# A fused attention and MLP kernel on one core: q and k cast by loads of GpSimd's queue, two more groups with seven quarter products, and a list planned anew

## The chip, the cores and the metric

The kernel runs on one core of a Trainium2 chip. The core has TensorE (PE; matmuls, with the weight load PEld beside them), VectorE (DVE), ScalarE (ACT), GpSimd (POOL) and SyncE (SP, which here only issues DMAs). Each takes its instructions in order, and they wait for each other by semaphores. Sixteen DMA engines move data between HBM and the on-chip memory SBUF; the loads are issued from the queues of SP, ACT and POOL. PSUM is the memory that TensorE writes. The metric is device microseconds of one execution; lower is better.

## The reference

Attention with a feature map, then an MLP with a residual. `phi` takes the largest magnitude off and gives two exponentials; the MLP normalises, multiplies by `w_ch1`, clips at zero, multiplies by `w_ch2`.

```python
def phi(x):                                  # x: 8 x 8 x 576 x 64
    proj = np.einsum('bhsd,df->bhsf', x, w_phi)          # 128 features
    proj = proj - np.max(np.abs(proj), axis=-1, keepdims=True)
    return np.concatenate([np.exp(proj), np.exp(-proj)], axis=-1)
q_p, k_p = phi(q), phi(k)
kv, z = np.einsum('bhsf,bhsd->bhfd', k_p, v), np.sum(k_p, axis=2)
num = np.einsum('bhsf,bhfd->bhsd', q_p, kv)
den = np.einsum('bhsf,bhf->bhs', q_p, z)[..., None] + 1e-06
x = (num / den) heads side by side                        # 8 x 576 x 512
xn = (x - mean) / np.sqrt(var + 1e-06) * g_ln
out = x + np.maximum(xn @ w_ch1, 0.0) @ w_ch2             # 512 -> 2048 -> 512
```

## The kernel before

Attention goes in 32 units of two heads of a batch each (units 0 to 31, eight to a pair of batches). A unit needs q, k and v as float32 from HBM: eight token tiles of 128 in the main part, and a ninth, mixed one from the tails of both heads. The main parts lie in three buffers `qk_100`, `qk_102`, `qk_104` (and `v_101`, `v_103`, `v_105`) of two units each, the tails in `qx_88`/`qx_89` and `vx_106`/`vx_107` of four units each.

TensorE needs q and k transposed and in bf16. For units 0 to 7 it transposes them itself. From unit 8 on `a_trans_dma` casts them to bf16 into one of three buffers `b16` (b_0, b_1, b_2, by the unit's number modulo 3), in two steps, `cast_mixed` for the tails and `cast_main` for the rest, on VectorE, ScalarE or GpSimd as the list says; then SyncE issues a transposing DMA into one of four buffers `qkT` (141 to 144). Then follow for each unit the projections `pm` and `pt`, the maxima `m`, the exponentials `ea` and `eb`, the scaled values `vv` (GpSimd: three instructions, lines 1101 to 1107), the product `kv` in the PSUM bank `n_bank` (lines 1162 and 1168), the numerators `num`, and the quotients `x` and `xs` (GpSimd).

The MLP goes in nine groups of four token tiles (0 to 8; `LAST` is 8), each as soon as its `x` is there. The first product `hT_ps` (`first`, and `first_half` in group 0) runs over 16 blocks of 128 of the 2048 features; each is clipped into `hT`. The second product of a group has two forms. `second` (line 1562) adds 16 blocks of 512 columns for each of four token tiles into one PSUM bank: 64 matmuls of 512 columns. `fast` (line 1698) is for the groups in `FAST`: a pair of token tiles by two halves of the columns would be eight quarter products, and it forms seven, from sums of `hT` blocks (`token_sums`, S1 to S4 of each pair) and of `w2` blocks (`weight_sums`, T1 to T4): 7 steps of 16/2 = 8 matmuls of 256 columns for each of two pairs, 112 in all. Each step's sum is read and added into the output tile `o` by VectorE (line 1707). With `second` a tile's result is one instruction, on VectorE (line 1570) or on ScalarE with a residual on GpSimd (lines 1575 and 1579). T lies in the buffers of q and k of units that are past, S likewise, for the second pair in those of v. Before, `FAST` is groups 6, 7 and 8.

The weights come by four loads of GpSimd's queue that cast them to bf16, each half a matrix (1 MB as written): two of `w1` (`w_132`, 4 KB rows), two of `w2` (`w_133`, 2 KB rows). The first loads of `w1` are gated on v of units 2 and 3; SyncE's loads for units 8 and up wait until the second half of `w1` has landed (`hold`).

What sets the order is a list of numbers for each engine, `ORDER`. `Order.run` plays the recorded steps against this list with assumed durations and lags, which decides how the engines' instructions interleave, and where TensorE is given filler matmuls (`wz`, of no use but to keep its clock up) in the first 75 us. The list was made by a planner that used the same assumed figures: `SLACK` (lags and a factor for DMAs), `LAG`, and in `dma` the time of a packet and the lag from its move to its landing.

Of the kernel before, what the change touches and what calls it, by code (L numbers as in the profile page):

```python
# [17 lines left out]
def bcast(ap: bass.AP, dim: int, n: int) -> bass.AP:  # L18
# [10 lines left out]
SLACK = ((0.22, 0.0, 0.0, 0.97), (0.35, 0.6, 1.6, 0.97), (0.22, -1.15, 0.0, 1.07))  # L29
# [36 lines left out]
    """,  # L66
    "SP": """
# [11 lines left out]
    """,  # L79
    "ACT": """  # L80
# [307 lines left out]
def kernel(  # L388
# [46 lines left out]
    BW = 4
# [1776 lines left out]
```

## Time and profile before

| | us |
|---|---|
| median of 3 runs | 354.47 |
| the runs | 352.18, 354.47, 355.43 |
| the profiled execution | 353.76 |
| its span, first to last instruction | 352.0 |
| mean granted clock of TensorE | 0.998 |

The rows that the prediction shows are not shown here. In a group's row stand the line, the engine, the operation, what it writes and reads, the shapes, the count, then busy time in us and the mean of one in ns, then the engine's idle time ahead of it and what ended that. In the chain of waits and in the timeline a row has the start and the duration in us. A row of stretches has for each engine its busy time and the number of its instructions in brackets.

### The profile page before, as it was taken

The page shows a single profiled execution, that of the slowest core. Times are in us where ns is not written, and L with a number is a line of the kernel's source. Part 1 is how long each engine was busy: PE and PEld are TensorE (multiplying, and loading weights), DVE is VectorE, ACT ScalarE, POOL GpSimd, SP SyncE. Part 2 cuts the span into 40 slices and gives each one's busy share as a digit, 9 for nine tenths or more (in the row PEclk, how much of TensorE's full clock was granted, in tenths as well). Part 3 has the DMA queues.
Part 4 walks back from the last instruction along what each step waited for, and adds up shares of the span by engine and source line. Part 5 has one row for each costly group of instructions (what it writes and reads, how often), then busy time and mean ns, then how long its engine had stood idle before and what let it go on. Part 6 is the DMA issues. An engine that isn't in the chain of part 4 may idle for free.

```text
span 352.0 us, 9056 instructions
## 1 busy us (share of the span) xinstructions
PE 339.7 (97%) x3482; PEld 216.1 (61%) x3482; DVE 296.1 (84%) x670; ACT 253.5 (72%) x561; POOL 192.7 (55%) x250
## 2 busy tenths in 40 slices
PE   8887998999999999999999999999999999999995
PEld 7766785655555555464555455555555578488884
DVE  5799984999889889878896799799768699999994
ACT  4997988878999887869776958798676840554410
POOL 5487367849952584667292696987668630000000
PEclk9999999999999999999999999999999999999999
DMA  7999999994997939859809993705061123500053
GB/s 206 277 297 214 212 236 232 254 198 58 266 270 183 248 96 216 160 105 209 281 16 190 284 281 64 136 0 125 10 128 58 62 67 61 148 33 3 7 114 119
DMA packets 93675, 53.87 MB, mean 153 GB/s; under 512 B 61104, under 2 KB 88048, under 8 KB 93632
## 3 DMA queue, kind: packets, MB, share of 16 engines
q1 hardware_dynamic: 89392, 47.72, 57.2%
q0 software_dynamic: 3328, 4.49, 7.4%
q10 hardware_dynamic: 912, 1.08, 0.9%
q8 instruction: 27, 0.44, 0.5%
q14 instruction: 16, 0.13, 0.1%
HBM read 36.77 MB, written 9.44 MB: 131 GB/s over the span
## 4 chain that ended last, share of the span: by engine, by line
PE 82%; DMA 8%; DVE 3%; issue 2%; POOL 2%; ACT 2%; SPq 1%; ACTq 0%; POOLq 0%
PE hT_ps L1530 27%; PE ch_ps L1562 23%; PE ch L1698 10%; DMA w<-in_moe_w_ch_dram 6%; PE pm L1017 4%; PE n_bank L1168 4%; PE sum L1881 3%; PE num L1226 3%; PE pt L1026 2%; DMA qk<-in_q_dram 2%; POOL vv L1101 1%; PE n_bank L1162 1%; PE n_bank L1226 1%; ACT ea L914 1%; PE n_bank L1232 1%
## 5 line engine op out<-in xcount | busy, mean ns | idle before, releaser
L1530 PE MATMUL hT_ps<-xT,w 128*128 128x512 bf16 x432 | 103.9, 380 | 0.0
L1562 PE MATMUL ch_ps<-w,hT 128*128 128x512 bf16 x384 | 89.7, 380 | 1.2 <-DMA w<-in_moe_w_ch_dram 1.2
L1101 POOL TENSOR_TENSOR vv<-v,ek 128x1024 bf16<-128x1024 f32 x32 | 61.2, 1912 | 49.6 <-issue 32.9
L1074 DVE TENSOR_REDUCE m<-pm 128x8 f32<-128x1024 f32 x60 | 72.3, 1214 | 14.2 <-PE pm L1017 13.1
L1094 ACT ACTIVATE eb<-pm 128x1024 bf16<-128x1024 f32 x64 | 64.5, 1044 | 4.8 <-DVE m L1074 3.0
L1138 ACT ACTIVATE ea<-pt 128x1024 bf16<-128x1024 f32 x56 | 56.1, 1045 | 11.1 <-PE pt L1026 10.9
L1530 PEld LDWEIGHTS <-w 128*128 128x128 bf16 x432 | 38.1, 97 | 39.2 <-issue 1.9
L1562 PEld LDWEIGHTS <-hT 128*128 128x128 bf16 x384 | 35.0, 97 | 39.8 <-issue 2.5
L1540 ACT ACTIVATE hT<-hT_ps 128x512 bf16<-128x512 f32 x64 | 37.7, 608 | 18.6 <-PE hT_ps L1530 18.4
L1293 POOL TENSOR_TENSOR x<-numc,rden 128x128 bf16<-128x128 f32 (+1 forms) x56 | 33.6, 615 | 18.6 <-DVE rden L1260 18.6
L1538 DVE TENSOR_SCALAR hT<-hT_ps 128x512 bf16<-128x512 f32 x44 | 29.7, 679 | 5.4 <-PE hT_ps L1530 5.2
L1226 PEld LDWEIGHTS <-ea 128*128 128x128 bf16 x448 | 21.6, 97 | 8.5 <-issue 0.3
L804 POOL TENSOR_TENSOR b<-qk,one 128x1024 bf16<-128x1024 f32 x13 | 24.5, 1890 | 2.3 <-DMA v<-in_v_dram 2.3
L1168 PE MATMUL n_bank<-vv,eb 128*128 128x65 bf16 x512 | 23.8, 194 | 0.0
L1168 PEld LDWEIGHTS <-eb 128*128 128x128 bf16 x512 | 21.3, 98 | 2.2
L1248 DVE TENSOR_TENSOR numc<-num,em 128x390 f32<-128x390 f32 (+1 forms) x32 | 17.0, 530 | 6.6 <-PE num L1226 5.9
L1434 DVE BATCH_NORM_STATS2 st<-x 128x6 f32<-128x512 bf16 (+1 forms) x40 | 21.9, 567 | 0.4 <-POOL x L1293 0.4
L1017 PE MATMUL pm<-wbk,qkT 64*128 64x128 bf16 x448 | 19.9, 218 | 0.2 <-DVE xT L962 0.2
L1107 POOL TENSOR_TENSOR vv<-vx,ek 128x260 bf16<-128x260 f32 x32 | 19.9, 623 | 0.0
L1017 PEld LDWEIGHTS <-qkT 64*128 64x128 bf16 x448 | 13.8, 94 | 9.6 <-issue 6.5
L1579 POOL TENSOR_TENSOR o<-o,x 128x512 f32<-128x512 f32 x13 | 15.0, 1158 | 7.8 <-ACT o L1575 6.9
L1254 DVE TENSOR_TENSOR numc<-numc,num 128x390 f32<-128x390 f32 (+1 forms) x32 | 17.0, 533 | 0.7
(180 smaller groups left out, 659.7 us busy)
## 6 DMA issues: line engine op xcount, KB each, us to landing
out_dram<-o SPq DMA_DIRECT2D x29, 256.0 KB, 3.1
qk<-in_q_dram SPq DMA_DIRECT2D x12, 512.0 KB, 5.6
qk<-in_k_dram SPq DMA_DIRECT2D x12, 512.0 KB, 6.4
v<-in_v_dram SPq DMA_DIRECT2D x12, 512.0 KB, 5.2
w<-in_moe_w_ch_dram POOLq DMA_DIRECT2D x4, 1024.0 KB, 10.4
qk<-in_k_dram SPq DMA_DIRECT2D x8, 256.0 KB, 6.1
qk<-in_q_dram SPq DMA_DIRECT2D x7, 256.0 KB, 5.9
v<-in_v_dram SPq DMA_DIRECT2D x7, 256.0 KB, 6.7
```

Of the source, the lines that this page charges most:

```text
L1017: nc.tensor.matmul(ps[:, half * 4 + c, :], u["qkT"][rows, cols], wbk[rows, half, :], start=True, stop=True,)
L1074: nc.vector.reduce_max(out=m, in_=ps, axis=AX.X, apply_absolute_value=True)
L1094: nc.scalar.activation(eb, ps, AF.Exp, scale=(1.0, -1.0)[t])
L1101: eng.tensor_tensor(out=u["vv"][:, :, 0:MX, 0:D], in0=bcast(vb[:, hh, :].rearrange("p (c d) -> p c d", d=D), 1, 2), in1=bcast(e[:, :, 0:MX ...
L1138: nc.scalar.activation(u["EA"][:, t, 0:1024], u["pt"], AF.Exp, scale=(1.0, -1.0)[t])
L1168: nc.tensor.matmul(ps[:, t, c // 4, :], EB[:, t, c, :], vv[:, t, c, :], start=False, stop=(t == 0 and c == MX - 1), skip_group_check=True,)
L1226: nc.tensor.matmul(ps[t][:, i, :], ea(u, t, c), KV[:, t, c // 4, :], start=True, stop=True,)
L1293: eng.tensor_tensor(out=dst, in0=src, in1=by, op=ALU.mult)
L1530: nc.tensor.matmul(st["ps"], w1_sb[:, kc, jj * P : (jj + 1) * P], xT_bufs[g % XB][:, kc::KC, :], start=(kc == 0), stop=(kc == KC - 1),)
L1540: nc.scalar.activation(h_sb, st["ps"], AF.Relu)
L1562: nc.tensor.matmul(ch[g, i], hT[g, jj][:, i * P : (i + 1) * P], w2_sb[:, jj, :], start=(jj == 0), stop=(jj == JC - 1),)
L1698: nc.tensor.matmul(sums(), left(c), right(c), start=(begin and c == 0), stop=(c == CP - 1), skip_group_check=True,)
```

## The change

Five things change.

First, from unit 8 on the main parts of q and k aren't loaded as float32 any more. `cast_main` goes, and two loads of GpSimd's queue for each unit, one for q and one for k (`load_cast`, line 830 of the new kernel), read 1 KB rows from HBM, cast them and write `b16` directly: 48 loads that read 256 KB each. SyncE's 24 loads of q and k for those units go. The tails are still loaded by SyncE and cast by `cast_mixed`. A `b16` buffer can only be loaded again when the transposing DMA of the unit three before has read it.

Second, `FAST` is groups 4 to 8. In groups 4 and 5 (`lean`) one pair is worked through after the other with a single set S, and its sums lie in two PSUM banks of the pool B: chains 0 and 1 share a bank, chain 2 has the other. In groups 6 to 8 nothing changes in this.

Third, a token sum can be done by GpSimd too, and the list gives it 44 of them.

Fourth, the planner's figures: DMA landings and transposes are assumed later (`SLACK`), the weights' loads land 4.4 and 4.7 us after they moved where it was 2.9, and their pieces move one load after the other.

Fifth, the whole list is planned anew; the first steps that differ are GpSimd's eighth and SyncE's fourteenth.

```diff
-SLACK = ((0.22, 0.0, 0.0, 0.97), (0.35, 0.6, 1.6, 0.97), (0.22, -1.15, 0.0, 1.07))
+SLACK = ((0.22, 0.6, 0.8, 1.0), (0.35, 1.2, 2.2, 1.0), (0.22, -1.15, 0.0, 1.07))
...
     "POOL": """
-        0 7 9 10 20 22 31 86 109 168 131 150 200 219 136 137 206 155 205 241 288 33 246 169 293
+        0 7 9 10 20 22 31 447 449 456 442 86 109 137 170 150 33 131 223 204 136 156 210 209 245
...
-    FAST = (LAST - 2, LAST - 1, LAST)
+    FAST = range(4, LAST + 1)
+    FULL = LAST - 2
...
-            packets, ns, lag = nbytes / row / 16, (0.155 if row == 4096 else 0.084), 2.9
+            packets, ns, lag = nbytes / row / 16, {4096: 0.155, 2048: 0.084}.get(row, 0.048), {4096: 4.4, 2048: 4.7}.get(row, LAND)
...
-        def cast_main(engine):
-            cast(
-                engine, b16[:, 0 : MX * P].rearrange("p (i f) -> p i f", i=2),
-                qk_bufs[u["g"] % NBUF][:, :, u["hh"], :],
+        def load_cast(i):
+            b, h, step = heads(u["pair"], u["i"], 0)
+            t = (q, k)[i]
+            nc.gpsimd.dma_start(
+                out=b16[:, i * 4 * P : (i + 1) * 4 * P].rearrange("p (a f) -> p a f", a=2),
+                in_=bass.AP(
+                    tensor=t.tensor, offset=t.offset + (b * H + h) * S * D,
+                    ap=[[4 * D, P], [S * D, 2], [1, 4 * D]],
+                ),
             )
...
-        add(("DVE", "ACT", "POOL"), (1.13, 0.937, 1.852), rank, cast_main, r=[*loaded(u, "q"), *loaded(u, "k")],
-            w=[("b16", n % NB16)])
-        dma("SP", rank, 0, turn, r=[("b16x", n % NB16), ("b16", n % NB16)],
+        for i in range(2):
+            dma("POOL", rank, 262144, lambda i=i: load_cast(i), w=[("b16" + "qk"[i], n % NB16)], us=0.7, row=1024)
...
+        dma("SP", rank, 0, turn, r=[("b16x", n % NB16), ("b16q", n % NB16), ("b16k", n % NB16)],
...
-                add("DVE", Port(0.335), (), lambda i=i, f=sums: f(i),
+                add(("DVE", "POOL"), (Port(0.335), 1.08), (), lambda e, i=i, f=sums: f(i, e),
...
+        lean = g < FULL
+        z = 0 if lean else p
...
+        if lean:
+            cols, bank = chain % 2 * FH, chain // 2
...
+        if lean:
+            took = ("B", 1) if i in (0, 3) and cs[0] == 0 else None
+            gave = ("B", 1) if i in (5, 6) else None
...
-    def fast_steps():
+    def fast_steps(lean=False):
         pairs_, h1, h2 = range(NM // 2), range(SH), range(SH, CP)
+        if lean:
+            return [
+                (p, i, cs) for p in pairs_
+                for i, cs in [(i, cs) for cs in (h1, h2) for i in range(2)]
+                + [(i, range(CP)) for i in range(2, 7)]
+            ]
...
-                for key in "kqv":
+                for key in "kqv" if m < QK_DMA else "v":
                     load_main(key, m + i, 1 if m < H else HG, rank, "SP")
```

Three places show what moves. The first is the start of GpSimd's queue, after the load of `gln`. Before, the first `vv` (units 0 and 1) follow:

```order
L658 DMA gln<-in_moe_g_ln_dram 128x4x1
L1101 TENSOR_TENSOR vv<-v_101,ek 128x2x8x64
L1106 CAST vv<-ek 128x2x8
L1107 TENSOR_TENSOR vv<-vx_106,ek 128x2x130
L1101 TENSOR_TENSOR vv<-v_101,ek 128x2x8x64
```

Now, at the same place:

```order
L670 DMA gln<-in_moe_g_ln_dram 128x4x1
L830 DMA b_0_145<-in_q_dram 128x2x256
L830 DMA b_0_145<-in_k_dram 128x2x256
L830 DMA b_1_146<-in_k_dram 128x2x256
L830 DMA b_2_147<-in_k_dram 128x2x256
L1118 TENSOR_TENSOR vv<-v_101,ek 128x2x8x64
```

Four cast loads (q and k of unit 9, k of units 10 and 8) stand ahead of all `vv` and of the four loads of the weights.

The second place is where the loads of `w2` are issued, with SyncE's queue at the same time. GpSimd before, from the first half of `w2` on (`vv` of units 4 and 5, then the second half, then a cast of unit 8):

```order
L688 DMA w_133<-in_moe_w_ch_dram 128x8x512
L986 TENSOR_TENSOR x<-xT_140 128x2x2x64
L1101 TENSOR_TENSOR vv<-v_105,ek 128x2x8x64
L1106 CAST vv<-ek 128x2x8
L1107 TENSOR_TENSOR vv<-vx_107,ek 128x2x130
L1101 TENSOR_TENSOR vv<-v_105,ek 128x2x8x64
L1106 CAST vv<-ek 128x2x8
L1107 TENSOR_TENSOR vv<-vx_107,ek 128x2x130
L688 DMA w_133<-in_moe_w_ch_dram 128x8x512
L804 TENSOR_TENSOR b_2_147<-qk_102,one 128x1024
```

GpSimd now:

```order
L700 DMA w_133<-in_moe_w_ch_dram 128x8x512
L1003 TENSOR_TENSOR x<-xT_140 128x2x2x64 x2
L1011 TENSOR_TENSOR xs<-xT_140 128x64
L700 DMA w_133<-in_moe_w_ch_dram 128x8x512
L1118 TENSOR_TENSOR vv<-v_105,ek 128x2x8x64
L1123 CAST vv<-ek 128x2x8
L1124 TENSOR_TENSOR vv<-vx_107,ek 128x2x130
L830 DMA b_2_147<-in_q_dram 128x2x256
L1118 TENSOR_TENSOR vv<-v_105,ek 128x2x8x64
```

The second half of `w2` moves ahead of `vv` of units 4 and 5, and the last load that unit 8 needs, its q, stands behind it. SyncE before, from v of unit 6 on (`v_101` is v of units 6 and 7 here, and the second one is unit 7's; the transposing DMA at the end is unit 8's):

```order
L577 DMA v_101<-in_v_dram 128x2x256
L577 DMA vx_106<-in_v_dram 64x4x64
L577 DMA qk_102<-in_q_dram 128x4x256
L577 DMA qx_88<-in_k_dram 64x4x64 x2
L577 DMA v_101<-in_v_dram 128x2x256
L577 DMA qx_88<-in_q_dram 64x4x64
L577 DMA qx_89<-in_k_dram 64x4x64
L577 DMA qk_102<-in_k_dram 128x4x256
L577 DMA qx_88<-in_q_dram 64x4x64
L577 DMA v_103<-in_v_dram 128x4x256
L823 DMA_TRANSPOSE qkT_141<-b_2_147 128x9x128
```

SyncE now:

```order
L589 DMA v_101<-in_v_dram 128x2x256
L589 DMA qx_88<-in_k_dram 64x4x64 x2
L589 DMA qx_88<-in_q_dram 64x4x64 x2
L840 DMA_TRANSPOSE qkT_141<-b_2_147 128x9x128
L589 DMA qx_89<-in_q_dram 64x4x64
L589 DMA v_101<-in_v_dram 128x2x256
L589 DMA vx_106<-in_v_dram 64x4x64
L589 DMA qx_89<-in_q_dram 64x4x64
L589 DMA vx_106<-in_v_dram 64x4x64
L840 DMA_TRANSPOSE qkT_142<-b_0_145 128x9x128
L589 DMA v_103<-in_v_dram 128x4x256
```

Unit 8's transpose now stands ahead of v of unit 7 and of v of unit 8.

The third place is VectorE at the second product of group 4. Before, a token tile's result of 512 columns stands among maxima (`m`) and statistics of attention:

```order
L1451 TENSOR_SCALAR xc_137<-x,mv 128x512
L1613 TENSOR_TENSOR qk_104<-w_133 128x1024
L1570 SCALAR_TENSOR_TENSOR o<-ch_ps,rstd,x 128x512
L1074 TENSOR_REDUCE m_118<-pm 128x2x4
L1074 TENSOR_REDUCE m_119<-pm 128x2x4 x2
L1570 SCALAR_TENSOR_TENSOR o<-ch_ps,rstd,x 128x512
```

Now (`ch_3979` and `ch_4047` are the two banks of the first pair, `ch_4101` the first of the second pair; each row on `ch` is the result of a step of 8 matmuls):

```order
L1091 TENSOR_REDUCE m_118<-pm 128x2x4
L1737 SCALAR_TENSOR_TENSOR o<-ch_3979,rstd,x 128x256
L866 TENSOR_REDUCE m_118<-n_bank 128x2
L1737 SCALAR_TENSOR_TENSOR o<-ch_4047,rstd,x 128x256
L1737 SCALAR_TENSOR_TENSOR o<-ch_3979,rstd,o 128x256
L1655 TENSOR_TENSOR qk_100<-hT 128x512 x3
L1737 SCALAR_TENSOR_TENSOR o<-ch_4101,rstd,x 128x256
L1737 SCALAR_TENSOR_TENSOR o<-ch_4047,rstd,o 128x256
```

A result of a bank now has to be read before the next but one step of TensorE, which adds to it.

More of the change, by code (lines that the diff above doesn't have):

```diff
@@ L561, in dma @@
             add(queue, took[0], rank, emit, r=r, w=(key, *w), acquire=lanes)
-            add(kind, took[1], rank, None, r=(key, *r), w=(*w, key), lag=1.45, release=lanes)
+            add(kind, took[1], rank, None, r=(key, *r), w=(*w, key), lag=1.9, release=lanes)
             return
-        add(queue, us, rank, emit, r=r, w=(key, *w), acquire=lanes, load=(kind, packets * ns))
+        wide_ = kind == "DMA_w" and pieces > 1
+        line = ["weights issued"] if wide_ else []
+        add(queue, us, rank, emit, r=r, w=(key, *w, *line), acquire=lanes, load=(kind, packets * ns))
+        for i in range(pieces if wide_ else 0):
+            add(kind, Move(packets / pieces, ns), rank, None, r=(key,), w=("weights moved", (key, "moved")))
+        if wide_:
+            add(kind, Move(0.01, ns), rank, None, r=(key, (key, "moved"), *r), w=(*w, key), lag=lag, release=lanes)
+            return
         for i in range(pieces):
@@ L827, in a_trans_dma @@
         rank = rk("trans", n)
-        add(("DVE", "ACT", "POOL"), (0.193, 0.189, 0.357), rank, cast_mixed, r=[*loaded(u, "q"), *loaded(u, "k")],
-            w=[("b16x", n % NB16)])
-        add(("DVE", "ACT", "POOL"), (1.13, 0.937, 1.852), rank, cast_main, r=[*loaded(u, "q"), *loaded(u, "k")],
-            w=[("b16", n % NB16)])
-        dma("SP", rank, 0, turn, r=[("b16x", n % NB16), ("b16", n % NB16)],
+        for i in range(2):
+            dma("POOL", rank, 262144, lambda i=i: load_cast(i), w=[("b16" + "qk"[i], n % NB16)], us=0.7, row=1024)
+        add(("DVE", "ACT", "POOL"), (0.193, 0.189, 0.357), rank, cast_mixed,
+            r=[*loaded(u, "q")[2:], *loaded(u, "k")[2:]], w=[("b16x", n % NB16)])
+        dma("SP", rank, 0, turn, r=[("b16x", n % NB16), ("b16q", n % NB16), ("b16k", n % NB16)],
             w=[("qxT", j), ("qkT", j, 0), ("qkT", j, 1), *[("T", j, i) for i in range(3)]], tiles=NT)
@@ L1617, in weight_sums, with token_sums @@
                     + [("T home", i // 2)], w=[("T2", i, c)])
-    def token_sums(g, c):
-        for p in range(NM // 2):
+    def token_sums(g, c, only=None):
+        for p in range(NM // 2) if only is None else (only,):
+            z = p if g >= FULL else 0
             def blocks(i, odd, p=p):
@@ L1625, in blocks, with sums @@
                 return space[:, s : s + 2 * SH - 1 : 2, (2 * p + i) * P : (2 * p + i + 1) * P]
-            def sums(i, p=p, blocks=blocks):
-                S1, S2, S3, S4 = [t[:, c : c + SH] for t in S_of[p]]
+            def sums(i, engine, z=z, blocks=blocks):
+                S1, S2, S3, S4 = [t[:, c : c + SH] for t in S_of[z]]
                 out_, a, b, op = (
@@ L1634, in sums @@
                 )[i]
-                nc.vector.tensor_tensor(out=out_, in0=a, in1=b, op=op)
+                eng = nc.vector if engine == "DVE" else nc.gpsimd
+                eng.tensor_tensor(out=out_, in0=a, in1=b, op=op)
             for i, reads in ((0, ()), (1, (0,)), (3, (1,)), (2, ())):
-                add("DVE", Port(0.335), (), lambda i=i, f=sums: f(i),
+                add(("DVE", "POOL"), (Port(0.335), 1.08), (), lambda e, i=i, f=sums: f(i, e),
                     r=[hkey[g, jj] for jj in range(2 * c, 2 * c + 2 * SH)]
-                    + [("S", p, j, c) for j in reads] + [("S home", p)], w=[("S", p, i, c)])
+                    + [("S", z, j, c) for j in reads] + [("S home", z)], w=[("S", z, i, c)])
     def fast(g, p, i, cs):
         t0, t1 = 2 * p, 2 * p + 1
+        lean = g < FULL
+        z = 0 if lean else p
         f1, f2 = slice(0, FH), slice(FH, DM)
@@ L1692, in products @@
         def products():
-            if split and i < 2 and cs[0] == 0:
+            if lean:
+                if i in (0, 3) and cs[0] == 0:
+                    ch[g, p, bank] = room_for("B")
+            elif split and i < 2 and cs[0] == 0:
                 ch[g, p, i] = room_for((tag0, tag1)[i])
@@ L1699, in products @@
                     sums(), left(c), right(c),
-                    start=(begin and c == 0), stop=(c == CP - 1), skip_group_check=True,
+                    start=(begin and c == 0 and not (lean and i == 1)), stop=(c == CP - 1), skip_group_check=True,
                 )
@@ L1715, in fast @@
         else:
-            r += [("S", p, s_key, c) for c in range(cs[0], cs[-1], SH)]
+            r += [("S", z, s_key, c) for c in range(cs[0], cs[-1], SH)]
         if t_key is None:
@@ L1748, in fast @@
             dma("SP", counts["V"], 262144, lambda: store(g, t, ch["o", g, t]), r=both)
-    b16_home = [[("b16x", i), ("b16", i)] for i in range(NB16)]
+    b16_home = [[("b16x", i), ("b16q", i), ("b16k", i)] for i in range(NB16)]
     qkT_home = [
@@ L1994, in moe @@
             weight_sums()
+        if g == FULL:
+            add("SP", 0.0, RELU, None, w=[*S_home[1], ("S home", 1)])
         if g == LAST:
@@ L2011, in moe @@
             if g - 1 in FAST:
-                steps = fast_steps()
+                steps = fast_steps(g - 1 < FULL)
                 until = min(len(steps), -(-(jj + 1) * len(steps) // 8))
-                for step in steps[done:until]:
-                    fast(g - 1, *step)
+                for step in range(done, until):
+                    if g - 1 < FULL and 2 * step == len(steps):
+                        for c in (0, SH):
+                            token_sums(g - 1, c, 1)
+                    fast(g - 1, *steps[step])
                 done = until
             if g in FAST and jj in (SH * 2, JC - 1):
-                token_sums(g, 0 if jj < JC - 1 else SH)
+                token_sums(g, 0 if jj < JC - 1 else SH, 0 if g < FULL else None)
             if g - 1 in FAST:
```

5 lines of the change are left out of this document (3 added, 2 removed), and 216 rows, old and new, of the table ORDER.

## The prediction

> **What bounds the kernel now.** I read the page's first part, then busy time by stretches, then TensorE's own waits, then the chain of waits. The page opens with the span and each engine's busy time:
>
> ```profile
> span 352.0 us, 9056 instructions
> PE 339.7 (97%) x3482; PEld 216.1 (61%) x3482; DVE 296.1 (84%) x670; ACT 253.5 (72%) x561; POOL 192.7 (55%) x250
> ```
>
> Busy time by stretches (start and end in us, then each engine, the granted clock, the DMA share):
>
> ```profile
> core 0: us, PE busy (x) PEld busy (x) DVE busy (x) ACT busy (x) POOL busy (x), PEclk, DMA share, GB/s
> 30.00:40.00 10.00, 7.88 (x113) 6.33 (x112) 9.96 (x28) 8.61 (x18) 6.20 (x10) 1.00 1.12 194
> 60.00:285.00 225.00, 224.99 (x2258) 122.59 (x2256) 188.74 (x397) 181.27 (x397) 152.80 (x190) 1.00 0.66 155
> ```
>
> TensorE's waits on the weights (us in total, times, longest):
>
> ```profile
> PE ch_ps L1562 <- DMA w<-in_moe_w_ch_dram: 1.2, 1, 1.2
> PE hT_ps L1387 <- DMA w<-in_moe_w_ch_dram: 0.6, 1, 0.6
> ```
>
> There are two regimes. From 60 to 285 us TensorE works 224.99 of 225 us at full clock (1.00), and nobody else is full: there the time is TensorE's work and nothing else. Before 60 us TensorE is short of work, VectorE is near full, and the DMA share stands above 1, that is, packets queue at all 16 engines. The two waits on the weights are early; no wait of TensorE is longer, and these are the ones that the change can reach. So the change is worth what it takes from TensorE's work, plus or minus what it does to those first 60 us, plus any new wait in the full stretch.
>
> **The change, part by part.**
>
> Second products. Two groups (4 and 5) change from 64 matmuls of 512 columns to 112 of 256 each.
>
> In the chain of waits (start, duration, what) 16 of the old kind take 3.45 us, so a group takes 4 x 3.45 = 13.80:
>
> ```profile
> 219.53 3.45 PE ch_ps L1562 x16
> ```
>
> The new kind already stands there for another group, 112 in 12.23:
>
> ```profile
> 285.39 12.23 PE ch L1698 x112
> ```
>
> Saved: 2 x (13.80 - 12.23) = **3.1 us**, all on the path, since TensorE has no gap there.
>
> What it adds elsewhere, by groups of instructions (busy, mean ns):
>
> ```profile
> L1707 DVE SCALAR_TENSOR_TENSOR o<-ch,rstd,o 128x256 f32<-128x256 f32 x18 | 8.2, 476 | 1.7 <-PE ch L1698 1.7
> ...
> L1635 DVE TENSOR_TENSOR qk<-hT 128x512 bf16<-128x512 bf16 x10 | 4.1, 417 | 0.0
> ...
> L1613 POOL TENSOR_TENSOR qk<-w,qk 128x1024 bf16<-128x1024 bf16 x4 | 8.5, 2123 | 0.0
> ...
> L1579 POOL TENSOR_TENSOR o<-o,x 128x512 f32<-128x512 f32 x13 | 15.0, 1158 | 7.8 <-ACT o L1575 6.9
> ...
> L804 POOL TENSOR_TENSOR b<-qk,one 128x1024 bf16<-128x1024 f32 x13 | 24.5, 1890 | 2.3 <-DMA v<-in_v_dram 2.3
> ...
> L475 POOL DMA_DIRECT2D qx<-in_q_dram x2 | 1.3, 656 | 0.0
> ...
> L688 POOL DMA_DIRECT2D w<-in_moe_w_ch_dram x2 | 1.8, 924 | 0.0
> ```
>
> VectorE gets 28 results of 256 columns (28 x 0.476 = 13.3 us) and loses 11 of its token sums (4.6) and some of its relus, casts and centerings; its total stays within some 3 us of 296. ScalarE loses ten casts and nine results and gains eight centerings of half the size: it gets lighter, and has room in the full stretch (181 of 225). GpSimd loses 13 casts (24.6), nine residuals (10.4) and two weight differences (4.2), and gains 44 token sums (half of 2.12, so 1.06 each: 46.6) and 48 loads to issue. Such an issue isn't in the trace; the nearest have 0.66 us (256 pieces, as here) and 0.92 (1024 pieces): I take 0.66, so 31.7. Net +39, to 232 us. About half of that falls in the full stretch (four loads stand ahead of it, and the sums of the last groups behind it): 152.8 + 20 of 225, 77%. That is hidden as long as the queue's waits stay short (second rival). SyncE loses 24 loads.
>
> The start: four cast loads go ahead of the weights. GpSimd sat idle there, in its longest wait, so issuing costs nothing:
>
> ```profile
> POOL vv L1101 <- ACT em L910: 6.8, 1, 6.8
> ```
>
> Moving does, since DMA is full. The DMA view for 4 to 24 us, then rows of the chain and of the timeline:
>
> ```profile
> DMA packets 7180, 5.73 MB, mean 286 GB/s; under 512 B 2258, under 2 KB 7111, under 8 KB 7177
> ...
> 28.73 9.94 DMA w<-in_moe_w_ch_dram
> ...
> 34.25 0.62 PE L1356 MATMUL xT_ps<-ident,xc 128*128 128x128 bf16 x8 [0.78 <-DVE xc L1451]
> 38.72 1.92 PE L1387 MATMUL hT_ps<-xT,w 128*128 128x256 bf16 x16 [0.63 <-DMA w<-in_moe_w_ch_dram]
> 40.47 0.22 PE L1162 MATMUL n_bank<-vv,eb 128*128 128x130 bf16 x1
> 40.79 0.22 PE L1162 MATMUL n_bank<-vv,eb 128*128 128x130 bf16 x1
> ```
>
> DMA moved 286 GB/s. Four loads read 1.05 MB: 3.7 us if they move as the plain loads do, 1.8 us if only what they write counts (half). I take 3.3, nearer the plain row, since their reads have its size. The second half of w1 then lands at 38.67 + 3.3 = 42.0. But the new order puts 1.7 us more TensorE work ahead of the matmul that waits for it: 8 matmuls of 256 columns (0.87), 18 of n_bank (two times 0.32, the distance between the two n_bank rows) and 4 transposes (0.2, by the row of 8 at 34.25). So TensorE is 3.3 - 1.7 = 1.6 us behind there. It gets back the wait for w2.
>
> ```profile
> 47.52 10.79 DMA w<-in_moe_w_ch_dram
> ...
> L688 POOL DMA_DIRECT2D w<-in_moe_w_ch_dram x2: 921/924/928, 32.9 to 47.5; - x2
> ...
> DMA to landing us min/median/max: 10.8/11.1/11.4
> ```
>
> The second half of w2 was issued at 47.52, behind two vv steps, and landed 10.79 later, at 58.31, which cost the 1.2 us. The first half went out at 32.9 and took 11.4, so it landed at 44.3, 5.7 behind w1: loads of this queue follow one another. Now both halves are issued before those vv steps and move right behind w1: 42.0 + 2 x 5.7 + about 1.5 for four small loads in between = 54.9, before TensorE gets there (57 to 58). Early net: +1.6 - 1.2 = **+0.4 us**. Bounds: 1.8 instead of 3.3 gives -0.8 (not lower than the work, which must still be done); 3.7 gives +0.8.
>
> Unit 8's q. Its cast load stands on GpSimd's queue behind the second half of w2, and by the row above lands behind it, at about 54.9 + 0.9 = 55.8. SyncE is in order: unit 8's transpose waits for it, and behind the transpose stands v of unit 7.
>
> ```profile
> qkT<-b SPq DMA_TRANSPOSE x24, 4.1
> v<-in_v_dram SPq DMA_DIRECT2D x1, 256.0 KB, 6.7
> ...
> 63.45 0.62 POOL L1107 TENSOR_TENSOR vv<-vx,ek 128x260 bf16<-128x260 f32 x1
> 64.67 0.23 PE L1162 MATMUL n_bank<-vv,eb 128*128 128x130 bf16 x1
> ```
>
> The first two rows give issue to landing (us), for a transpose and for unit 7's v. Before, vv of unit 7 ended at 64.07, 0.6 us before TensorE took it: that is the tight place. Now v is issued near 58, and lands at 62 if the emptier queue takes 4 us, at 65 if it takes the 6.7 of the row. vv takes 2.6 more, its signal half a microsecond; TensorE is there at about 65. Wait: 0 to 3.1; I take **+0.8**, as the DMA has little else left then.
>
> Results of the new second products. In groups 4 and 5 a token pair has two PSUM banks whose steps alternate, 8 matmuls (0.87 us) each; step 4 adds to what step 2's result must have read. (In the three old groups two pairs alternate over four banks.)
>
> ```profile
> L1074 DVE TENSOR_REDUCE m<-pm 128x8 f32<-128x1024 f32 x60 | 72.3, 1214 | 14.2 <-PE pm L1017 13.1 <-PE pm L1011 0.9
> ...
> 328.33 1.04 PE L1698 MATMUL ch<-w,qk 128*128 128x256 bf16 x8
> 329.41 0.48 DVE L1707 SCALAR_TENSOR_TENSOR o<-ch,rstd,o 128x256 f32<-128x256 f32 x1 [0.49 <-PE ch L1698]
> 331.40 0.68 DVE L1898 TENSOR_TENSOR late<-sum,qx 128x512 bf16<-128x512 f32 x1
> 332.14 0.61 PE L1881 MATMUL sum<-ea,qkT 128*128 128x256 bf16 x4
> ```
>
> A result starts 0.04 us after its matmuls' end, lasts 0.48, and TensorE follows 0.06 after: 0.58, so 0.29 of slack if VectorE is free; a maximum (L1074) of 1.21 us stands right ahead of one of them. Four pairs, 0 to 0.5 each; I take 0.15 each, **+0.6**.
>
> Sum: -3.1 + 0.4 + 0.8 + 0.6 = -1.3. The profiled execution took 353.76 us (span 352.0, 1.76 around it); 353.76 - 1.3 = **352.4 us**. The median of the runs is 354.47, 0.7 above the profiled one, and the runs spread over 3 us; about 1% (3.5 us) is what a measurement of this kernel tells from no change.
>
> The replanned list also has 22 more filler matmuls early; they stand where TensorE has nothing to do, and cost nothing there.
>
> A rule that speaks against the change: by the Trainium skill, "SBUF — State Buffer", section "SBUF: two separate sides", GpSimd can't write the descriptors of its loads while VectorE holds the port they share, in its faster modes. The trace shows no such stretching: the two w2 issues took 0.92 us each with VectorE busy all around, though no run shows 48 of them beside centerings. If every second issue met a VectorE step of 0.42 us, GpSimd would lose 10 us of the 52 it has free: no time by itself.
>
> **The rivals.**
>
> *The start is free.* If the four loads move at what they write, or the new list fills the wait, the early term is -0.8 and the tight places cost nothing: 353.76 - 3.1 - 0.8 = 349.9. For it: the later transposes and landings were planned later. Against: DMA share above 1 from 10 us on. It decides when w1's second half lands before 41. Chance 0.25.
>
> *GpSimd's queue falls behind.* A cast load at its head waits until the buffer's last transpose is read; vv stands behind it, and TensorE takes vv 0.6 us after its end at the tight place. A wait of 0.9 us ahead of each of 24 vv would show 0.3 on TensorE: 7.2 us, 352.4 + 7.2 = 359.6, slower than before. It decides from about 0.8 us per unit. For it: 77% busy, in order. Against: SyncE's transposes land in 4 us and three buffers serve units that come every 9 us. Chance 0.12.
>
> *The tight places cost their upper bounds.* v of unit 7 3.1 and the pairs 2.0: 352.4 + 2.3 + 1.4 = 356.1. Chance 0.13.
>
> **How the numbers follow.** My forecast, 350.5 to 354, has 0.5. The range 349.4 to 356.5 takes in the first rival and the third, and leaves out the second and half a tenth below. Faster by over 1% (under 350.9) is most of the first rival and the edge of the forecast: 0.26. Slower by over 1% (over 358.0) is the second: 0.12. Within: 0.62.
>
> **What would show it.** The chain's 112 matmuls in 12.2 us twice more, and the ch_ps group at 256; w1's second wait at 41 to 43 us; no wait on w2; v of unit 7 landing after 60 and a wait of n_bank on vv near 65; waits of ch on VectorE in 165 to 230 us of under a microsecond. Wrong would be: TensorE idle over 3 us after 70 us, or GpSimd's cast issues much over 0.7 us.

## The result: 1.2 to 1.6% slower, and the profile after

| | before | changed |
|---|---|---|
| median, first comparison | 354.0 us (4 runs) | 358.42 us (4 runs: 355.53, 358.09, 358.75, 360.59) |
| ratio | | 1.0124, 95% interval 1.0078 to 1.0171 |
| median, timed a second time | 353.79 us (17 runs) | 359.52 us (6 runs, 356.49 to 360.37) |
| ratio | | 1.0156, 1.0125 to 1.0186 |
| profiled execution, its span | 353.76, 352.0 | 355.53, 353.8 |
| mean granted clock over the runs | 0.997 to 1.000 | 0.989 to 0.995, one run at 1.000 (the fastest but one, 356.49) |

The forecast was 352.4, with a range of 349.4 to 356.5. The time lies above the range, on the slower side. The execution that was profiled first is the fastest of all ten; a second profile, of an execution of 359.01 us, shows what the usual ones lose.

The page of the changed kernel opens so (busy time, share of the span, instructions):

```profile
span 353.8 us, 9397 instructions
PE 339.7 (96%) x3600; PEld 227.8 (64%) x3600; DVE 303.8 (86%) x671; ACT 245.9 (70%) x557; POOL 241.4 (68%) x320
```

TensorE's waits in it (us in total, times, longest):

```profile
PE xT_ps L1346 <- DVE xc L1468: 1.5, 1, 1.5
PE qkT_ps L742 <- DMA qk<-in_q_dram: 1.5, 2, 1.2
PE ch L1728 <- DVE o L1737: 1.2, 3, 0.6
...
PE qkT_ps L742 <- DMA qk<-in_k_dram: 0.7, 1, 0.7
```

The two waits on the weights are gone, and four others are there: for loads of q and k at the start, for one centering of VectorE, and for the results of the new second products. The timeline gives the places (start, duration, and in brackets the idle time ahead):

```profile
17.57 0.40 PE L742 MATMUL qkT_ps<-ident,qk 128*128 128x128 bf16 x4 [0.70 <-DMA qk<-in_k_dram]
19.21 0.40 PE L742 MATMUL qkT_ps<-ident,qk 128*128 128x128 bf16 x4 [1.24 <-DMA qk<-in_q_dram]
...
24.85 0.47 SPq L589 DMA_DIRECT2D qk<-in_q_dram  x1
24.92 0.82 POOL L682 DMA_DIRECT2D w<-in_moe_w_ch_dram  x1
```

The first two rows are k and q of unit 3. Behind these two waits the clock drops, as the stretches show (start and end, length, TensorE's busy time and matmuls, granted clock, DMA share, GB/s):

```profile
19.00:20.30 1.30, 1.09 (x23) 1.00 1.20 284
20.30:23.70 3.40, 3.26 (x33) 0.50 1.09 324
23.70:25.00 1.30, 1.30 (x32) 0.99 0.77 192
```

For 3.4 us TensorE ran at half its clock, which is 1.7 us of work. Yet this dip isn't what the usual execution loses. The execution that has it is the fastest of the ten, and the second profile, 3.5 us longer, doesn't have it:

```profile
20.00:21.00 1.00, 0.99 (x27) 1.00 1.18 261
21.00:22.00 1.00, 0.59 (x9) 1.00 1.13 275
22.00:23.00 1.00, 1.00 (x20) 1.00 1.09 342
23.00:24.00 1.00, 0.81 (x16) 1.00 1.10 349
```

The other two rows of the timeline show the load of q of unit 5 going out 0.07 us ahead of the first half of w1. Here it landed at 31.30 and TensorE waited 0.2 us for it. In the second profile it went out 0.70 behind w1, at 25.31. The chain of waits of that execution (start, duration), then TensorE's waits, then its stretches:

```profile
25.31 8.45 DMA qk<-in_q_dram
```

```profile
PE qkT_ps L742 <- DMA qk<-in_q_dram: 5.0, 3, 3.6
```

```profile
30.00:33.80 3.80, 0.22 (x4) 1.00 1.11 241
33.00:34.30 1.30, 0.49 (x13) 1.00 1.12 282
34.30:37.70 3.40, 3.40 (x49) 0.50 1.14 225
```

The load took 8.45 us, TensorE stood nearly still from 30 to 33.8, and behind that the clock dropped for 3.4 us. Compared matmul for matmul, this execution is 2.5 us behind the first one when the load has landed, and 3.6 when the dip is over.

Is it all at the start? A mark helps: the first transpose of group 1's `x` (`xT_ps` from `xc_137`), which all profiles have. Kernels that share the changed kernel's list from there on must take the same time behind it.

| profiled execution | reaches the mark at | from there to the end |
|---|---|---|
| before | 76.24 us | 275.8 us |
| changed, first profile | 76.88 | 276.9 |
| changed, second profile | 80.38 | 276.8 |
| with the loads late (below) | 75.94 | 276.9 |

Behind the mark the changed kernel takes 276.9 us, whether the execution lasts 355.5 or 359 us. What differs between the two executions lies ahead of it. And behind it the kernel is 1.1 us slower than before, although its second products have 3.1 us less work.

### The profile page after: what moved, and what is told of

It reads as the page before. It is cut to its first block, busy times and chain, and to the rows that moved or that the text cites. A ratio compares the mean times of both kernels' runs of the same rounds, so it can differ in the third digit from the quotient of the medians.

```text
span 353.8 us, 9397 instructions
## 1 busy us (share of the span) xinstructions
PE 339.7 (96%) x3600; PEld 227.8 (64%) x3600; DVE 303.8 (86%) x671; ACT 245.9 (70%) x557; POOL 241.4 (68%) x320
## 4 chain that ended last, share of the span: by engine, by line
PE 76%; DVE 13%; DMA 5%; POOL 2%; issue 2%; ACT 1%; ACTq 0%; SPq 0%; DVEq 0%
PE hT_ps L1547 24%; PE ch_ps L1579 14%; PE ch L1728 14%; PE pm L1034 4%; PE sum L1911 3%; DMA qk<-in_q_dram 3%; PE hT_ps L1404 3%; PE n_bank L1185 3%; DVE m L1091 3%; PE num L1243 3%; DVE st L1451 2%; PE pt L1043 2%; DVE o L1737 2%; DMA v<-in_v_dram 1%; DVE xc L1468 1%
## 5 line engine op out<-in xcount | busy, mean ns | idle before, releaser
L1118 POOL TENSOR_TENSOR vv<-v,ek 128x1024 bf16<-128x1024 f32 x32 | 61.0, 1906 | 36.5 <-issue 21.3
L1111 ACT ACTIVATE eb<-pm 128x1024 bf16<-128x1024 f32 x64 | 63.4, 1037 | 6.6 <-DVE m L1091 5.8
L1579 PE MATMUL ch_ps<-w,hT 128*128 128x512 bf16 x256 | 60.4, 379 | 0.0
L1155 ACT ACTIVATE ea<-pt 128x1024 bf16<-128x1024 f32 x56 | 55.1, 1037 | 4.1 <-PE pt L1043 4.0
L1557 ACT ACTIVATE hT<-hT_ps 128x512 bf16<-128x512 f32 x69 | 41.3, 613 | 20.9 <-PE hT_ps L1547 20.8
L1579 PEld LDWEIGHTS <-hT 128*128 128x128 bf16 x256 | 23.0, 98 | 24.4 <-issue 0.8
L1555 DVE TENSOR_SCALAR hT<-hT_ps 128x512 bf16<-128x512 f32 x39 | 26.3, 678 | 3.2 <-PE hT_ps L1547 3.0
L1728 PEld LDWEIGHTS <-hT 128*128 128x128 bf16 x216 | 20.9, 98 | 4.4 <-issue 1.3
L1728 PEld LDWEIGHTS <-qk 128*128 128x128 bf16 x224 | 21.5, 98 | 2.6 <-issue 0.2
L1728 PE MATMUL ch<-qk,qk 128*128 128x256 bf16 x168 | 20.7, 272 | 0.1
L1124 POOL TENSOR_TENSOR vv<-vx,ek 128x260 bf16<-128x260 f32 x32 | 20.3, 636 | 0.0
L1655 POOL TENSOR_TENSOR qk<-hT 128x512 bf16<-128x512 bf16 x11 | 13.1, 1191 | 10.4 <-ACT hT L1956 9.6
```

Source lines behind the costliest of these rows:

```text
L1111: nc.scalar.activation(eb, ps, AF.Exp, scale=(1.0, -1.0)[t])
L1118: eng.tensor_tensor(out=u["vv"][:, :, 0:MX, 0:D], in0=bcast(vb[:, hh, :].rearrange("p (c d) -> p c d", d=D), 1, 2), in1=bcast(e[:, :, 0:MX ...
L1155: nc.scalar.activation(u["EA"][:, t, 0:1024], u["pt"], AF.Exp, scale=(1.0, -1.0)[t])
L1557: nc.scalar.activation(h_sb, st["ps"], AF.Relu)
L1579: nc.tensor.matmul(ch[g, i], hT[g, jj][:, i * P : (i + 1) * P], w2_sb[:, jj, :], start=(jj == 0), stop=(jj == JC - 1),)
L1728: nc.tensor.matmul(sums(), left(c), right(c), start=(begin and c == 0 and not (lean and i == 1)), stop=(c == CP - 1), skip_group_check=True,)
```

## The experiments

Each kernel was timed in alternation with the kernel before; the ratio is to that. The changed kernel's code is taken, and one or more things are edited; the order of TensorE, and the fillers, stay as they are unless said.

**The changed kernel once more.**

> The changed kernel itself, timed beside the next three. Its profiled execution took 355.53 us at a mean granted clock of 0.995, its three other runs 358 to 361 at 0.989 to 0.990. Theory A (the clock): in the profile TensorE waits 0.70 and 1.24 us at 17 to 19 us for k and q of unit 3, whose loads are made late by the four early cast loads, and from 20.65 to 23.64 us the granted clock stands at 0.50; in the slower runs this dip is longer or comes twice. It expects a median of 357 to 359 and clocks between 0.988 and 0.995, the slower runs with the lower clock. Theory B (the middle of the kernel): the runs differ by waits after 75 us, and the clock has no part in it; it expects runs that differ by 3 us at one and the same clock.

359.52 us, 1.0156 (1.0125 to 1.0186). The clocks of its runs: 0.990, 0.990, 0.990, 0.995, 0.995 for 359.0 to 360.4 us, 1.000 for 356.49. The lower clocks lie with the longer times, as theory A expects, but they don't set them: at a clock of 1.000 the kernel is still 2.7 us above before, and the fastest execution of all, 355.53 us, had 0.995. The mechanism of theory A is not borne out either: the profiled execution here took 359.01 us without the dip at 20 us. (Finer stretches put the dip at 20.3 to 23.7, not 20.65 to 23.64.)

**Fillers where TensorE waits for unit 3.**

```diff
             for i in which:
+                for _ in range((24, 12)[i] if u["n"] == 3 else 0):
+                    nc.tensor.matmul(
+                        ps.bitcast(FP32)[:, i * 256 : i * 256 + WN], wz, wz[:, 0:WN],
+                        start=True, stop=True, skip_group_check=True,
+                    )
                 for c in range(4):
                     nc.tensor.transpose(
```

> The changed kernel with 36 more filler matmuls of 120 columns on TensorE, 12 ahead of the transposes of unit 3's k and 24 ahead of those of its q, just where it waits for these loads. The loads stay late. Theory A expects the clock at 1.00 from 20 to 24 us, 0.997 to 0.998 over the execution in all runs, and a median 2 to 4 us under the changed kernel's. Theory B expects the same median within 1 us. If it is the late loads themselves that cost the time, and not the clock, the median stays within 1 us too.

356.03 us, 1.0066 (1.0047 to 1.0084), 3.5 us under the changed kernel beside it. The clocks are 0.999 to 1.000 in five of six runs; the sixth, which the ratio leaves out, took 361.68 us at 0.991. So useless work at this place gains 1%, but that it does so by taking away the dip at 20 us isn't shown. At 24 us TensorE is 1.1 us ahead of the changed kernel's first profile, and at unit 5's q that lead is gone (0.4 behind). The loads stay late: q of unit 5 went out at 24.79, 0.24 us behind w1, and TensorE still waited 1.8 us for it. What is missing against the second profile is the wait of 3.6 us and the dip behind that one. How the fillers bring this about stays open.

**The four cast loads behind w2.** On GpSimd's queue:

```diff
-        0 7 9 10 20 22 31 447 449 456 442 86 109 ...
+        0 7 9 10 20 22 31 86 109 ...
...
-        ... 177 274 440 309 ...
+        ... 177 274 442 440 447 449 456 309 ...
```

> The changed kernel with the four early cast loads moved on GpSimd's queue from ahead of the first vv to behind the second half of w2 and the vv of unit 4, with unit 8's q second among the five; all else in its place. Theory A expects q of unit 3 to land by 18 us, no dip of the clock, the second half of w1 landing 2 to 3.5 us earlier (37.5 to 39), and a median of 353 to 355. Theory B expects it within 1 us of the changed kernel. A third way: the loads land too late behind w2, unit 9's and 10's transposes wait, and TensorE waits for qkT at 60 to 75 us; then it is 1 to 4 us slower than by theory A.

353.12 us, 0.9989 (0.9970 to 1.0007): 5.9 to 6.4 us less than the changed kernel (by the ratios 0.0167 of 353.8, and by the medians), and as fast as before. q of unit 3 landed at 16.80 instead of 19.16, and the clock stayed at 1.00. The second half of w1 landed at 40.10 instead of 41.03, only 0.9 us earlier, against the 2 to 3.5 expected. So w1 is not the way in which the loads cost. q of unit 5 went out at 22.86, still 0.12 us ahead of w1, landed at 30.13, and TensorE waited 1.65 us for it.

**Unit 5's q first.** On SyncE's queue:

```diff
-        ... 52 50 70 64 68 58 ...
+        ... 52 50 68 70 64 58 ...
```

> The changed kernel with one load moved on SyncE's queue: q of unit 5, ahead of v of units 4 and 5 instead of behind them; the four early cast loads stay where the change put them. In the changed kernel's profiles this load is issued beside the first half of w1 (24.85 beside 24.92; 25.31 behind 24.61) and lands at 31.30 or 33.76, and TensorE waits for it 0.4 us in the one and 3.6 us in the other. Theory D (a load that meets w1): it lands by 29 us, TensorE waits for it under 0.5 us, the clock has no dip at 33 to 38 us, and the median is 355 to 356.5, with the runs closer together. Rival: the four cast loads delay everything, this load too, and its place among the loads hardly matters; then the median stays over 358.

355.10 us, 1.0052 (1.0029 to 1.0075); clocks 0.998 to 1.000 in eleven of twelve runs. The load went out at 23.32 and landed at 28.47, in time. The wait for unit 3 is as long as ever (1.38 us at 18.77), but nothing comes after it.

**Both.**

> Both edits: the four early cast loads behind the second half of w2, and q of unit 5 ahead of the two v. With the cast loads alone moved, the median was 353.1, and TensorE still waited 1.6 us at 30.18 for q of unit 5. Theory D expects that wait to be under 0.3 us and a median of 351.3 to 352.4. Rival: TensorE then waits for the next late thing (w1, or x of group 0), and the median stays at 352.7 to 353.5.

353.17 us, 0.9976 (0.9956 to 0.9996). q of unit 5 went out at 20.90 and landed at 25.84, and there is no wait for it. Over the late loads alone the gain is 0.1%, less than expected and inside the rival's 352.7 to 353.5; the intervals overlap. Either edit takes away the wait of 3.6 us, so together they give little more.

**The same loads in the kernel before.** Behind its load of `gln`:

```diff
             nc.gpsimd.dma_start(out=gln_sb, in_=moe_g_ln.rearrange("(kc p) -> p kc", p=P))
+            for t, n, i in ((q, 9, 0), (k, 9, 1), (k, 10, 1), (k, 8, 1)):
+                b, h, step = heads(n // H, n % H, 0)
+                nc.gpsimd.dma_start(
+                    out=b16_bufs[n % 3][:, i * 4 * P : (i + 1) * 4 * P].rearrange(
+                        "p (a f) -> p a f", a=2),
+                    in_=bass.AP(
+                        tensor=t.tensor, offset=t.offset + (b * H + h) * S * D,
+                        ap=[[4 * D, P], [S * D, 2], [1, 4 * D]],
+                    ),
+                )
```

> The kernel before, with four loads added on GpSimd's queue behind the load of gln: the same four cast loads (q and k of unit 9, k of units 10 and 8, 1.05 MB read) that the change puts there, into the b16 buffers; nothing reads what they write, and the casts overwrite it. If the loads' place is what costs the changed kernel its start (theory A and D), SyncE's loads behind them land 2 to 4 us later here too, q of unit 5 (issued 21.3 us before) goes out next to the first half of w1, and the median rises by 1.5 to 4.5 us. Rival (the order of SyncE's queue alone is to blame): within 0.7 us of the kernel before.

357.88 us, 1.0123 (1.0099 to 1.0146): the old kernel is made 4.4 us slower by four loads that nobody reads. (The expectation's 21.3 us is the issue of unit 7's q; unit 5's went out at 18.82 in the kernel before.) TensorE's waits in it:

```profile
PE qkT_ps L740 <- DMA qk<-in_q_dram: 2.2, 2, 1.5
PE qxT_ps L748 <- DMA qx<-in_q_dram: 1.2, 1, 1.2
```

q of unit 3 landed at 19.43, 15.17 before; its last q went out at 25.56 instead of 21.34; the clock stood at half from 20.6 to 24. The wait of 1.1 us on w2 is there as before. Of the 4.4 us between the two profiles 3.2 lie ahead of the mark (79.43 against 76.24); the other 1.2 come between 96 and 99 us, and why stays open. With the late loads above, this is the same cause put in and taken out.

**One centering, a miss.** An edit of the list moved a number from VectorE to ScalarE.

> The changed kernel with one centering of group 1 (the one that took 2.45 us on VectorE at 76.24, where the same form has a median of 0.35) moved to ScalarE. Theory C (the shared port): VectorE's instruction, which reads and writes bf16, stood still while GpSimd ran two xs and then a vv, from 76.24 to 78.36; without it TensorE's wait of 1.69 us at 78.75 falls to between 0.2 and 0.9 (ScalarE takes 0.7 for it), and the time falls by 0.8 to 1.5 us at the same clock. A rival: the centering was late for its input, and on ScalarE TensorE waits as long as before.

The number was the wrong one: it belongs to a centering of group 2, and the one of 2.45 us stayed where it was, with TensorE's wait of 1.5 us behind it. So this run says nothing of theory C. It took 361.18 us, 1.0214 (1.0194 to 1.0234); in its profile q of unit 5 went out 0.54 us behind w1 and landed 10.2 later, and the clock was at 0.51 for 6.9 us. A centering on ScalarE that wasn't needed cost 1.0 us behind the mark (277.9).

**The right centering on ScalarE**, with both edits of the loads. Number 548 goes from VectorE's list to ScalarE's, behind 546.

> Those two edits, and the centering of group 1 that takes 2.45 us on VectorE (beside GpSimd's vv) moved to ScalarE, behind ScalarE's own centering of that group. Theory C (the shared port) expects TensorE's wait of 1.5 us for it to fall to 0.2 to 0.9, and the median 0.7 to 1.4 us under that with two edits. Rival (late input): the wait stays above 1.2 us and the median within 0.4.

352.44 us, 0.9957 (0.9939 to 0.9974), 0.7 us under the two edits; TensorE's wait fell from 1.5 to 0.4 us, and the time behind the mark from 276.9 to 275.8. Theory C holds so far, at the lower edge of its numbers.

**GpSimd's vv out of the way**, from the two edits; the centering stays on VectorE.

```diff
-        ... 476 537 639 664 ...
+        ... 476 639 537 664 ...
```

> The kernel with two edits (late cast loads, q of unit 5 first); the centering stays on VectorE, but GpSimd does its vv of that place behind the next x instead of ahead of it. Theory C (the shared port): with GpSimd idle there, the centering takes 0.3 to 0.6 us instead of 2.45, TensorE's wait of 1.5 us at 77 us falls under 0.3, and the median falls by 1.0 to 1.7 us, more than with the centering on ScalarE. Rival: it is slow by itself (late input, or its form) and stays above 1.5 us; or vv is late for TensorE's product of K, which then waits over 0.5 us at 81 us.

351.64 us, 0.9945 (0.9928 to 0.9962), 1.1 us under the two edits by the ratios, and 0.55% under the kernel before: the fastest complete kernel that was run, with the next. TensorE doesn't wait for a centering there, and the time behind the mark is 275.7 us. In the changed kernel GpSimd and VectorE stood so (start, duration):

```profile
75.95 0.55 POOL L1314 TENSOR_TENSOR xs<-numc,rden 128x64 bf16<-128x64 f32 x2
76.24 2.45 DVE L1468 TENSOR_SCALAR xc<-x,mv 128x512 bf16<-128x512 bf16 x1
76.46 1.90 POOL L1118 TENSOR_TENSOR vv<-v,ek 128x1024 bf16<-128x1024 f32 x1
78.75 0.45 PE L1346 MATMUL xT_ps<-ident,xc 128*128 128x128 bf16 x5 [1.52 <-DVE xc L1468]
```

And here VectorE's same two centerings:

```profile
72.75 0.56 DVE L1468 TENSOR_SCALAR xc<-x,mv 128x512 bf16<-128x512 bf16 x1
73.52 0.42 DVE L1468 TENSOR_SCALAR xc<-x,mv 128x512 bf16<-128x512 bf16 x1
```

The form is the same, the input too; without a vv beside it the centering takes 0.42 instead of 2.45 us. It ended at 78.69, that is 0.33 behind vv's end at 78.36, and 0.33 is about what such a centering takes alone. So it did nothing until that vv was through. The xs alone hardly hold it: here too the second xs runs beside the centering (from 73.49 to 73.78).

**Another share of the PSUM banks.** In the first pair of groups 4 and 5 chain 1 goes beside chain 2:

```diff
-            cols, bank = chain % 2 * FH, chain // 2
-            took = ("B", 1) if i in (0, 3) and cs[0] == 0 else None
+            cols, bank = (chain // 2 * FH, min(chain, 1)) if p == 0 else (chain % 2 * FH, chain // 2)
+            took = ("B", 1) if i in (0, 3 - 2 * (p == 0)) and cs[0] == 0 else None
```

> Those three edits, and in the first pair of groups 4 and 5 chain 1 shares its PSUM bank with chain 2 instead of chain 0; the second pairs stay as they are. Theory E (the shared bank): the half step (1, h2) of TensorE waits until VectorE has read chain 0's sum, since both lie in one bank and nothing stands between them; this is the wait of 0.57 us at 215.83 and of 0.41 at 252.85 in the changed kernel. It expects both to be gone in the first pairs (under 0.2 us), those of the second pairs to stay, and the median 0.6 to 1.3 us lower. Rival (a busy VectorE): the result comes late because VectorE stands in other work, the waits stay or move to the next step, and the median stays within 0.4.

351.70 us, 0.9947 (0.9930 to 0.9964). Against three edits that is 0.1% by the ratios, within their intervals, where 0.6 to 1.3 us were expected, and the profiled spans are 351.1 and 351.0. The waits were at these places in the changed kernel:

```profile
213.78 1.47 PE L1728 MATMUL ch<-w,hT 128*128 128x256 bf16 x12
...
215.29 0.48 DVE L1737 SCALAR_TENSOR_TENSOR o<-ch,rstd,x 128x256 f32<-128x256 f32 x1
...
215.83 0.60 PE L1728 MATMUL ch<-w,hT 128*128 128x256 bf16 x4 [0.57 <-DVE o L1737]
```

Twelve matmuls, then a stop until VectorE has read chain 0, then the four that are left of chain 1 in the same bank. With the banks shared otherwise the sixteen run through (1.91 us), and the wait stands a step later:

```profile
214.38 1.19 DVE L1091 TENSOR_REDUCE m<-pm 128x8 f32<-128x1024 f32 x1
...
215.48 0.48 DVE L1737 SCALAR_TENSOR_TENSOR o<-ch,rstd,x 128x256 f32<-128x256 f32 x1
...
216.01 1.03 PE L1728 MATMUL ch<-qk,qk 128*128 128x256 bf16 x8 [0.41 <-DVE o L1737]
```

Now a maximum of 1.19 us stands ahead of the next result. Theory E names the place rightly, but taking the place away gained next to nothing.

**Without the token sums of groups 4 and 5**, from three edits and from four.

```diff
-                eng.tensor_tensor(out=out_, in0=a, in1=b, op=op)
+                eng.tensor_tensor(out=out_, in0=a, in1=b, op=op) if g >= FULL else None
...
-            return lambda c: S_of[z][n][:, c, :]
+            return (lambda c: S_of[z][n][:, c, :]) if not lean else A(t0 + n % 2, n // 2)
```

> The kernel with three edits (late cast loads, q of unit 5 first, the centering on ScalarE), without the token sums of groups 4 and 5: the 32 sums on VectorE and GpSimd are left out, and the products read blocks of hT in their place, in the same number and shape. Theory E (the shared bank): the waits on the sum of chain 0, 0.5 to 0.7 us at 213 and 250 us, stay, since VectorE reads that sum at once; the other waits of these groups may go; gain 0.3 to 1 us. Theory G (VectorE has too much to do there, the token sums and their meeting GpSimd's included): all of them go, gain 1.5 to 2.5 us against the kernel with three edits (352.4).

> The same without the 32 token sums, from the kernel with four edits (chain 1 beside chain 2 in the first pairs). If E and G both hold, the waits at 211 to 217 and 248 to 252 us are all under 0.25 us here, and only those of the second pairs are left: 349.6 to 350.6. If VectorE's maxima (1.2 us each) are what stands ahead of the results, the wait of 0.41 us that this kernel has at 216 us stays, and it is within 0.4 of the same kernel with chain 1 beside chain 0.

351.36 us, 0.9939 (0.9923 to 0.9956), and 351.30, 0.9935 (0.9917 to 0.9953). I added up by how much TensorE's matmuls from 205 to 285 us start later than at the median distance of their form (those over 0.12 us late). That gives nothing in the kernel before, and 2.7 us in the changed kernel, in that with three edits and in that with four; without the sums it gives 2.2 and 2.0. So the sums cost 0.5 to 0.7 of the 2.7. With three edits the two waits on the shared bank are what they were (0.74 and 0.57 us late), so theory E is right about them. With four edits they are gone, and 0.58 and 0.55 us stand at 216 and 251 in their place: the first behind the maximum, which the missing sums don't change, the second on ScalarE's `ea`. Theory G falls: most of the loss isn't the sums.

In the changed kernel the 2.7 us lie at seven places. Three are results of the new products (0.74, 0.28 and 0.57 us late, 1.6 in all). The other four are matmuls of attention, three of `n_bank` (0.35, 0.21 and 0.19) and one of `num` (0.34), 1.1 in all; TensorE's waits put one of them down to ScalarE's `ea` and one to its `eb`. Why these four come late stays open.

## Why the prediction was wrong

**The step that failed** is "The start", and in it the sentence "Moving does, since DMA is full". It let the four cast loads delay one thing, the second half of w1, and gave 3.3 us for that. That half landed at 41.03, 2.4 later than before, and no matmul waited for it in any profile but that of the kernel before. What the loads did delay was SyncE's own loads of q and k (q of unit 3 landed at 19.16 instead of 15.17), which were not priced at all. SyncE lets its next load go when an older one has landed (k of unit 3 landed at 17.53 and the next went out at 17.55; q at 19.16, the next at 19.18), so the delay is handed on through the queue until q of unit 5 meets w1 (before, it went out at 18.82, 4.7 us ahead of w1). TensorE transposes units 0 to 7 itself and waits for each of these loads directly. The second half of the failure is the clock, of which the prediction says nothing: behind the wait of 3.6 us for that load it stood at half for 3.4 us, and that added 1.1 us to the 2.5 that the load came later than in the first profile. The dip at 20 us left no such loss in the changed kernel. Put in and taken out, the four loads are worth 4.4 us (kernel before with them) and 5.9 us (changed kernel without them at that place). Predicted for the start: +0.4.

**SyncE's order.** v of units 4 and 5 stand ahead of unit 5's q, as they did before (numbers 70 and 64, then 68, in SyncE's list); the new list puts k of unit 5 and k and q of unit 7 (66, 144 and 146) ahead of it as well. The prediction looked at this queue only around unit 8. The place behind the two v alone is worth 3.7 us (1.0156 to 1.0052), as long as the four loads are early.

**Second products, −3.1.** Right as work. The chain of waits has, in group 4,

```profile
217.24 5.69 PE ch L1728 x52
```

that is 0.1094 us each, 112 in 12.25. But 2.7 us of the 3.1 came back as late starts in the same stretch, 1.6 at the results and 1.1 at attention's matmuls.

**Results on VectorE, +0.6 (0 to 2.0).** Mis-sized, within its bounds: 1.6. The term took the alternation to be of whole steps of 8 matmuls, with 0.29 us of slack. The first two steps are split in halves, and chain 0's last half stands right ahead of chain 1's in one bank, with nothing between; the slack there is nil, and the 0.58 us worked out for a result stands in full. The 1.1 us at attention's matmuls has no term at all; the full stretch was taken to stay free of waits but for the results.

**w2, −1.2.** Right: its second half landed at 52.80 (54.9 predicted), and from 40 to 60 us TensorE's only wait is this:

```profile
PE xT_ps L1373 <- DVE xc L1468: 0.2, 1, 0.2
```

**Unit 8's q, +0.8.** The mechanism is right, the price nil. Its load went out at 40.89 and landed at 53.47, behind w2; but v of unit 7 went out at 55.72 and landed at 59.23, in 3.5 us, earlier than the 62 taken, and no wait of n_bank stood near 65.

**GpSimd.** 232 us and 77% of 60 to 285 were predicted; it is 241.4, and 174.7 of these 225 (78%). An issue takes 0.74 to 0.76 us, not 0.66, and a token sum 1.15 to 1.34 by its form, not 1.06:

```profile
L830 POOL DMA_DIRECT2D b<-in_q_dram x24 | 18.1, 755 | 0.1
L830 POOL DMA_DIRECT2D b<-in_k_dram x24 | 17.7, 744 | 0.0
L1655 POOL TENSOR_TENSOR qk<-hT,qk 128x512 bf16<-128x512 bf16 x11 | 13.2, 1208 | 0.1
```

The first two rows end with the idle time ahead of these 48 issues, 0.1 us in all: no load waited for its buffer. The queue didn't fall behind, so the second rival isn't what made it slower. The rule on the shared port was weighed in one direction, VectorE stopping GpSimd's issues; no issue took over 0.774 us, and no run here shows that. The other direction, GpSimd stopping VectorE, was not looked for, and cost 1.5 us at 78.75.

**The sum.** For the profiled execution: ahead of the mark +0.6 (76.88 against 76.24: w2's wait gone, the clock and the waits for q and k come); behind it −3.1 of work, +2.7 of late starts in groups 4 and 5, +1.5 for the centering, 1.1 in all. 352.0 + 0.6 + 1.1 is 353.7, as measured (353.8). The usual execution adds 3.5 ahead of the mark (80.38). That the first profile's +0.6 lies near the predicted +0.4 is luck: nothing waited for w1, and in other executions the same loads cost far more.

**"What would show it."** The 112 matmuls, no wait on w2, and 256 rows of ch_ps came true. So did waits of ch under a microsecond from 165 to 230 us (0.6), but that window leaves out group 5, with 0.4 more at 253. w1's second wait at 41 to 43, v of unit 7 after 60 and a wait of n_bank on vv near 65 did not come. The text named TensorE idle over 3 us after 70 us as a sign against it, and that came: from 60 to 285 us it was busy 221.85 of 225, so 3.15 idle, where it was 0.01 before.

## What to carry to other kernels

A load put early into a full DMA can be paid by the loads behind it on another queue, here SyncE's, and most by the one that then meets a large transfer: look for the consumer with the least slack, not for the largest transfer. A dip of the clock needn't cost what it lasts: the one at 20 us here was taken up before the next load that TensorE needed. So compare executions with and without a dip before calling it the cause. Before work is given to GpSimd, look at which long two-operand steps of it will stand beside bf16 steps of VectorE that TensorE waits for.

## What the runs showed of the hardware

The clock fell to 0.50 for 3.4 us (20.3 to 23.7) behind two waits of 0.70 and 1.24 us with 0.4 us of transposes between them. It fell likewise behind 0.40 and 1.46 us (the kernel before with the four loads), but not behind 0.19 and 1.38 (q of unit 5 first). It did not fall behind single waits of 1.65 and 1.8 us at 30 to 32 us in two other runs; it fell for 3.4 us behind one of 3.6, and stood at 0.51 for 6.9 us behind one of 5.2. The Trainium skill, "TensorE: Matmul & The Clock Gate", section "HAM oscillation — how this bites in real kernels", gives the rule "no PE-idle gaps >~3.4µs". The dip behind the gap of 3.6 us agrees with it. The first dip here came with no gap over 1.3 us, so the trace puts the limit lower, where the gaps come close together.

A VectorE step that reads and writes bf16 stood still through a whole vv of GpSimd, 2.45 to 2.46 us in each profile that has the pair; beside an xs alone it took 0.42. The Trainium skill, "SBUF — State Buffer", section "Who interferes with whom", says that whoever comes first has the shared pair for the whole instruction and the other blocks. The trace agrees in that the wait lasts for the whole instruction. It doesn't show who comes first: the centering's row starts at 76.24, ahead of vv's at 76.46, and yet vv went through first.

A 256 KB load beside a 1 MB cast load: q of unit 5 took 6.45 us when it went out 0.07 us ahead of w1, 7.3 at 0.12 ahead, 6.9 at 0.24 behind, 8.45 at 0.70 behind, 10.2 at 0.54 behind; 4.9 and 5.2 when it went out 3.0 and 1.2 us ahead.
